# Centring the first block's tiles on VectorE before the turn, one mean from ScalarE, and a new order of the first loads, in an S5 + GEGLU layer

## The chip, the cores and the metric

The kernel runs on one core of one Trainium2 chip. Its engines are TensorE (PE; its weight loads are shown apart as PEld), VectorE (DVE), ScalarE (ACT), GpSimd (POOL) and SyncE (SP), which here only issues transfers. The metric is the device time of one execution in microseconds (us), the median of several runs.

## What is computed

One layer norm feeds two branches that are added to the input. `x` is 2048 x 512 in bf16. Cut to what matters:

```python
xn = (x - mean(x)) / sqrt(var(x) + eps)              # per row
dt = exp(log_dt); Lam_bar = exp(dt * Lam)            # 512 complex states
Bu = xn @ B_bar.T                                    # B_bar = ((Lam_bar - 1) / Lam) * B
h[t] = Lam_bar * h[t-1] + Bu[t]                      # scan over the 2048 rows
y = 2 * real(h @ C.T) + xn * Dskip
g = (gelu(xn @ w_gate) * (xn @ w_up)) @ w_down       # 512 -> 1376 -> 512
out = x + y + g
```

## The kernel before

The rows of x are cut into four blocks of 512 and each block into four tiles of 128 rows. Blocks 1 to 3 go one way: statistics and normalisation on VectorE, a transpose by DMA (`TR`), then matmuls with the transposed block: `GU` (gate and up), `BU` (into the states), the scan on VectorE (`CHAIN`) and `DN` (down projection and output).

Block 0 is handled apart so that TensorE has work early. Its gate and up products for the first 896 of the 1376 hidden columns (`GT_mm`, L693, matmuls at L703) use tiles that are only centred and turned on TensorE itself, not by DMA. The scale 1/std of a row is applied afterwards, as the factor `sc` of the gelu on ScalarE (L712) and of the product on VectorE (L715). The rest of block 0 uses the ordinary transposed block (`TR(0)`, L727, four DMA transposes issued on SP; then `GU(0)`, L828).

How tiles of block 0 were turned: for tiles 0 and 1 `raw_T` (L669) multiplies the uncentred tile by an identity, and `center` (L675) adds, in the same PSUM bank, a 512-column matmul of ones with a diagonal of negative means (`diag`, L928, on VectorE). Tiles 2 and 3 are centred on VectorE (`sub`, L932) and then turned by four PE transposes (`cent_T`, L686). In all cases ScalarE copies the turned tile out of PSUM to `XC` (L661). Ahead of this TensorE runs ten dummy matmuls of 512 columns (L918).

A tile's statistics are two VectorE instructions: L616 (bn_stats) and L617 (bn_aggr). `root` (L622 on VectorE, L623 and L624 on POOL) and `recip` (L628) make 1/std for two tiles at a time. `norms` (L635) writes the fully normalised tiles over the centred ones, and `TR(0)` waits for them.

The order on an engine comes from a scheduler inside the program: every operation is listed with a duration and its buffers, priorities are worked out backwards, and each engine's queue is fixed at build time. TensorE and SP keep the order of the listing. `ch` chains VectorE's first operations in a written order. A field `nb` forbids the scheduler to place an operation before a given time.

The first loads: SP issues the x tiles 0, 1 and 2, the first up chunk (columns 0 to 383), x tile 3, then the second and third gate and up chunks. ScalarE's queue issues the first gate chunk and three 1 KB parameter rows (L505). `load_par` (L519) on SP transposes the parameter rows after they have landed; its result feeds `params` (POOL's pow at L557 and the VectorE operations after it). Behind it on SP come the fourth gate and up chunk, `TR(0)`, x of block 1, the transposes of B, and so on. ScalarE also loads its table and runs a dummy gelu (L544) before its first copy.

Of the kernel before, what the change touches and what calls it, by code (L numbers as in the profile page):

```python
# [361 lines left out]
def d_pe(n_list):  # L362
    return sum(n / 2.4 + 2.5 for n in n_list)
# [3 lines left out]
def d_dve_ts4x(n): return 220.0 + 0.26 * n  # L367
D_TINY = 160.0
def d_act(n, ptr=0): return 190.0 + 0.833 * n + 90.0 * ptr
# [3 lines left out]
def build(nc, ins, out):  # L373
    with ExitStack() as es:
# [8 lines left out]
        def ring(parent, name, n):  # L383
            return [A.sub(parent, "%s%d" % (name, i), i) for i in range(n)]
# [74 lines left out]
        XCs = [[Buf("XC%d_%d" % (j, n), "xc", 2 * j + n, 2 * j + n + 1) for n in range(2)] for j in range(4)]  # L459
        ONE = A.alloc("ONE", [128], BF16, at=XC_all.hi)  # L460
        DG_all = A.alloc("DG", [2, 128], BF16, at=ONE.hi); DG = ring(DG_all, "DG", 2)
        H0_all = A.alloc("H0", [4, 896], BF16, at=SSb[2].lo); H0 = ring(H0_all, "H0_", 4)
# [15 lines left out]
        V(lambda e: e.memset(WRM.ap, 0.0), 150, [], [WRM], "wrm")  # L478
        half = V(lambda e: e.memset(HALF.ap, 0.5), D_TINY, [], [HALF], "half")  # L479
        V(lambda e: e.memset(PROW16.ap, 0.0), D_TINY, [], [PROW, *PROWq], "prow0")  # L480
        V(lambda e: e.memset(ONE.ap, 1.0), 250, [], [ONE], "one")

# [5 lines left out]
        def ld_w(W, Wc, src, ci, queue="sync", after=()):  # L488
            f0, f1 = FCH[ci]
            return S.dma(lambda e: e.dma_start(W.ap[:, :, f0:f1], src[:, f0:f1].rearrange("(k p) f -> p k f", p=128)),  # L490
                         512 * (f1 - f0) * 2, writes=[Wc[ci]], tag="ld_w", queue=queue, after=after)

        def ld_x0(j):
            S.dma(lambda e, j=j: e.dma_start(X[j].ap, x2[128 * j:128 * (j + 1), :]), 128 * 1024, writes=[X[j]], tag="ld_x0")
        ld_x0(0)
        ld_x0(1)
        ld_w(WG, WGc, ins["B_w_gate"], 0, "scalar", [half])
        ld_x0(2)
        ld_w(WU, WUc, ins["B_w_up"], 0)
        ld_x0(3)  # L500
        for ci in (1, 2):
            ld_w(WG, WGc, ins["B_w_gate"], ci)
            ld_w(WU, WUc, ins["B_w_up"], ci)
        for q, (nm, nb) in enumerate((("A_log_dt", 900.0), ("A_Lambda_re", 1300.0), ("A_Lambda_im", 1600.0))):
            S.dma(lambda e, q=q, nm=nm: e.dma_start(PROW.ap[4 * q:4 * q + 4, :], ins[nm].rearrange("(s p) -> s p", p=128)),  # L505
                  1024, writes=[PROWq[q]], tag="ld_" + nm, queue="scalar").nb = nb
        def late_loads():
# [5 lines left out]
        def load_T(bufs, nms):  # L513
            for b_, nm in zip(bufs, nms):
                S.dma(lambda e, b_=b_, nm=nm: e.dma_start_transpose(b_.ap, ins[nm]),
                      1.2 * 512 * 1024, writes=[b_], tag="tr_" + nm, issue=3000.0)

        def load_par():
            S.dma(lambda e: e.dma_start_transpose(PAR.ap.rearrange("p q t -> p (q t)").unsqueeze(1), PROW16.ap), 4096,  # L519
                  reads=PROWq, writes=[PAR], tag="tr_par", issue=900.0)  # L520

# [17 lines left out]
        POOL(lambda e: e.memset(HPI.ap, 0.5 * math.pi), 100, [], [HPI], "hpi")  # L539
        POOL(lambda e: e.iota(IOT.ap, [[1, 128]], base=0, channel_multiplier=-1), 300, [], [IOT], "iota")  # L540
        V(lambda e: e.tensor_scalar(IDN.ap, IOT.ap, 0.0, None, ALU.is_equal), d_dve_ts4x(128), [IOT], [IDN], "ident")
        POOL(lambda e: e.iota(IOTJ.ap, [[1, 512]], base=0, channel_multiplier=0), 600, [], [IOTJ], "iotj")
        SCR = A.alloc("SCR", [1], F32)
        ACT(lambda e: e.activation(SCR.ap, HALF.ap[:, 0:1], ACTF.Gelu_apprx_tanh), 200, [HALF], [SCR], "gelu0").nb = 1900.0  # L544
        POOL(lambda e: e.memset(HR.ap, 0.0), 300, [], HRp, "hr0")
        rstate = {"n": 0}
# [21 lines left out]
        W16p = [A.sub(A.alloc("W16v", [4, 4], F32, at=W16.lo), "W16_%d" % i, i) for i in range(4)]  # L568
        GATE = {"before_gelu": [], "nh": 0}
        sinT, sinP, cosT, cosP = (SC16.ap[:, 4 * i:4 * i + 4] for i in range(4))  # L570
# [82 lines left out]

        def xc_evac(j, bank, src, engs, after=()):
            for n, eng in enumerate(engs):
                per = KD // len(engs)
                dst = XC_all.ap[:, per * n:per * (n + 1), 128 * j:128 * (j + 1)]
                sr = src[:, 128 * per * n:128 * per * (n + 1)].rearrange("p (q t) -> p q t", q=per)
                w = [XCs[j][n]] if len(engs) == 2 else XCs[j]
                if eng == "A":  # L660
                    GATE["evTA"] = ACT(lambda e, sr=sr, dst=dst: e.activation(dst, sr, ACTF.Copy), d_act(128 * per), [BANK[bank]], w, "evT", after)  # L661
                else:
                    GATE["evT"] = V(lambda e, sr=sr, dst=dst: e.tensor_copy(dst, sr), 110 + 0.6 * 128 * per, [BANK[bank]], w, "evT", after)

        def raw_T(j, bank):
            def f(e):
                ins_ = None
                for k in range(KD):
                    ins_ = e.matmul(PS[bank][:, 128 * k:128 * (k + 1)], X[j].ap[:, 128 * k:128 * (k + 1)], IDN.ap,  # L669
                                    start=(k == 0), stop=False, skip_group_check=True)  # L670
                return ins_
            PE(f, 56.0 * KD, [X[j], IDN], [BANK[bank]], "T0")

        def center(j, bank, engs):
            PE(lambda e: e.matmul(PS[bank][:, :].rearrange("p (q t) -> p q t", q=KD), ONE.ap,  # L675
                                  DG[j].ap.unsqueeze(1).broadcast_to([128, KD, 128]), start=False, stop=True, skip_group_check=True),
               d_pe([512]), [ONE, DG[j], BANK[bank]], [BANK[bank]], "T0c")
            xc_evac(j, bank, PS[bank], engs)

        def cent_T(j, bank):  # L680
            pt = PS[bank].bitcast(BF16)

            def f(e):
                ins_ = None
                for k in range(KD):
                    ins_ = e.transpose(pt[:, 128 * k:128 * (k + 1)], XN[j].ap[:, 128 * k:128 * (k + 1)], IDN.ap)  # L686
                return ins_
            PE(f, 56.0 * KD, [XN[j], IDN], [BANK[bank]], "T0")
            xc_evac(j, bank, pt[:, 0:512], "A")

        FR = ((0, 192), (192, 384), (384, 640), (640, 896))

        def GT_mm(j, r, bank, us, ks=range(KD)):  # L693
            f0, f1 = FR[r]
            w = f1 - f0
            ci = max(0, r - 1)
            Wc = [(WGc, WUc)[u][ci] for u in us]
            dst = PS[bank][:, w * us[0]:w * (us[-1] + 1)].rearrange("p (w f) -> p w f", w=len(us))

            def f(e):  # L700
                ins_ = None
                for k in ks:
                    ins_ = e.matmul(dst, XCd(j, k), WGU[:, us[0]:us[-1] + 1, k, f0:f1], start=(k == 0), stop=(k == KD - 1))  # L703
                return ins_
            PE(f, d_pe([w * len(us)] * len(ks)), Wc + XCs[j][ks[0] // 2:ks[-1] // 2 + 1], [BANK[bank]], "GT")
# [204 lines left out]

        nwarm = 10
        wrm4 = WRM.ap.unsqueeze(1).broadcast_to([128, 4, 128])
        wb = next_bank()

        def fwarm(e, wb=wb):
# [3 lines left out]
            return ins_  # L919
        PE(fwarm, d_pe([512] * nwarm) * 1.6, [WRM], [BANK[wb]], "warm")  # L920
        tb = [next_bank(), next_bank()]
        tail_op = [None]

        def ch(*ops):
            for op in ops:
                tail_op[0] = S.order_behind(op, tail_op[0])
        def diag(j):
            return V(lambda e: e.tensor_scalar(DG[j].ap, IDN.ap, MVt[0][j].ap[:, 0:1], -1.0, ALU.mult, ALU.mult),  # L928
                     d_dve_ts4x(128), [IDN, MVt[0][j]], [DG[j]], "dg")

        def sub(j):
# [3 lines left out]
        load_W()  # L935
        for j in range(2):
            ch(*stats(0, j)); ch(diag(j))
        op, mn0, qb0, rq0 = root(0, 0, 2)
# [8 lines left out]

        raw_T(0, tb[0])
        center(0, tb[0], "AA")
        raw_T(1, tb[1])  # L950
        ub = {(j, r): next_bank() for j in range(2) for r in range(2)}
        for ks in ((0, 1), (2, 3)):
            for r in range(2):
                GT_mm(0, r, ub[0, r], [0], ks)
        center(1, tb[1], "A")
        def unit(j, r):
            bank = next_bank()
            GT_mm(j, r, bank, [0, 1])
            GT_evac(j, r, bank, rss[j])
        for j in range(2):  # L960
            if j:
                for r in range(2):
                    GT_mm(j, r, ub[j, r], [0])
                cent_T(2, tb[0])
            for r in range(2):
                GT_mm(j, r, ub[j, r], [1])
                GT_evac(j, r, ub[j, r], rss[j])
        unit(2, 0); unit(2, 1)
        unit(0, 2)
        cent_T(3, ub[0, 0])  # L970
        unit(1, 2)
# [97 lines left out]
```

## Time and profile before

| what | us |
|---|---|
| median of 7 runs | 179.28 |
| lowest and highest of them | 178.97, 179.51 |
| the profiled execution | 178.73 |
| its span, first to last instruction | 177.2 |
| TensorE busy in the span | 173.3 |
| VectorE busy | 159.0 |
| ScalarE busy | 88.8 |
| first GT matmul starts | 5.66 |
| first matmul of GU(0) starts | 18.88 |

Times inside the profile count from the start of the span. The chain of waits is followed back from the last instruction; each row names the engine, the line and how long the chain stayed there. A row of the timeline has the start, the time taken, engine and line, what is written and read, how many instructions are merged, and in brackets the idle time before it and what ended it. `ACTq` and `SPq` are the instruction queues that issue transfers; a transfer's landing comes later than its issue. The granted TensorE clock is 1.000 in the whole profile; matmuls at the very start are nevertheless seen twice as far apart as later ones of the same size.

### The profile page before, as it was taken

To read this page: it belongs to the slowest core of one execution; us is meant where nothing else is said; L and a number is where in the kernel's file an instruction comes from. 1 tells how busy PE (TensorE), PEld (TensorE's weight loads), DVE (VectorE), ACT (ScalarE), POOL (GpSimd) and SP (SyncE) were. 2 spreads that over 40 slices of the span, in tenths; PEclk is the share of its full clock that TensorE was granted. 3 is DMA by queue.
4 is the path that set the end of the run, shared out by engine and by line. 5 is a ranking of instruction groups with operands and counts; after the bars stand their busy time and mean duration, and the time that the engine had idled before them with its cause. 6 is when DMAs were issued, how large, how long until landed. Compare 5 with 4: busy or idle time off the path is not lost.

```text
span 177.2 us, 2501 instructions
## 1 busy us (share of the span) xinstructions
PE 173.3 (98%) x887; PEld 83.9 (47%) x887; DVE 159.0 (90%) x285; ACT 88.8 (50%) x167; POOL 10.1 (6%) x24
## 2 busy tenths in 40 slices
PE   7999999999999999999999999999999999999994
PEld 3754464444644444444644444444454444444453
DVE  4989999897999999779999999989999999999711
ACT  3475578998776898003676694000677770000000
POOL 3330240200000000300000000000000000000000
PEclk9999999999999999999999999999999999999999
DMA  5999986595999000011025000100001000000401
GB/s 156 334 298 108 251 232 125 96 153 110 147 252 304 0 4 2 0 52 67 4 41 107 0 2 0 33 30 30 30 0 30 4 0 0 0 0 30 139 31 43
DMA packets 33380, 14.36 MB, mean 81 GB/s; under 512 B 23672, under 2 KB 33368, under 8 KB 33368
## 3 DMA queue, kind: packets, MB, share of 16 engines
q1 hardware_dynamic: 32816, 13.81, 34.0%
q10 hardware_dynamic: 552, 0.40, 0.8%
q8 instruction: 7, 0.11, 0.3%
q14 instruction: 5, 0.04, 0.1%
HBM read 6.46 MB, written 2.10 MB: 48 GB/s over the span
## 4 chain that ended last, share of the span: by engine, by line
PE 98%; DVE 0%; ACT 0%; issue 0%
PE PS L868 37%; PE PS L828 32%; PE PS L739 16%; PE PS L703 7%; PE PS L802 3%; PE PS L918 2%; PE PS L686 0%; PE PS L675 0%; ACT arena L661 0%; DVE arena L886 0%; PE PS L669 0%; DVE arena L478 0%; DVE arena L479 0%
## 5 line engine op out<-in xcount | busy, mean ns | idle before, releaser
L868 PE MATMUL PS<-arena 128*128 128x512 bf16 (+3 forms) x323 | 66.2, 366 | 0.0
L828 PE MATMUL PS<-arena 128*128 128x512 bf16 x264 | 58.1, 379 | 0.0
L868 PEld LDWEIGHTS PS<-arena 128*128 128x128 bf16 (+1 forms) x323 | 30.8, 98 | 35.2
L828 PEld LDWEIGHTS PS<-arena 128*128 128x128 bf16 x264 | 25.8, 98 | 30.4
L772 DVE TENSOR_TENSOR_SCAN arena<-arena 128x512 bf16<-128x512 f32 x32 | 38.7, 1251 | 0.0
L843 ACT ACTIVATE arena<-PS 128x512 bf16<-128x512 f32 x33 | 19.8, 601 | 37.1 <-PE PS L828 32.6
L739 PE MATMUL PS<-arena 128*128 128x512 bf16 x128 | 28.1, 379 | 0.0
L846 ACT ACTIVATE arena<-PS 128x512 bf16<-128x512 f32 x33 | 19.8, 601 | 4.8 <-PE PS L828 4.7
L739 PEld LDWEIGHTS PS<-arena 128*128 128x128 bf16 x128 | 12.5, 98 | 14.9
L886 DVE TENSOR_TENSOR arena<-PS,arena 128x512 bf16<-128x512 f32 (+2 forms) x17 | 10.8, 652 | 8.9 <-PE PS L868 8.9
L860 ACT ACTIVATE PS<-arena 128x512 f32<-128x512 bf16 (+2 forms) x17 | 9.3, 581 | 17.4 <-DVE arena L886 16.7
L743 ACT ACTIVATE arena<-PS 128x512 bf16<-128x512 f32 x32 | 17.3, 595 | 1.3 <-PE PS L739 1.3
L848 DVE TENSOR_TENSOR arena<-arena 128x512 bf16<-128x512 bf16 x33 | 13.1, 411 | 1.7 <-ACT arena L846 1.7
L703 PE MATMUL PS<-arena 128*128 128x192 bf16 (+2 forms) x80 | 13.1, 315 | 0.4 <-ACT arena L661 0.3
L616 DVE BATCH_NORM_STATS2 arena<-arena 128x6 f32<-128x512 bf16 x16 | 10.2, 680 | 1.7 <-DMA arena<-in_A_x_dram 1.7
L759 DVE TENSOR_TENSOR arena<-arena 128x4096 bf16<-128x4096 bf16 (+1 forms) x5 | 9.2, 1858 | 0.7 <-ACT arena L611 0.7
L703 PEld LDWEIGHTS PS<-arena 128*128 128x128 bf16 x80 | 7.0, 98 | 5.6 <-ACT arena L661 0.7
L761 DVE TENSOR_TENSOR arena<-arena 128x4096 bf16<-128x4096 bf16 (+1 forms) x5 | 9.2, 1857 | 0.0
L785 DVE TENSOR_TENSOR arena<-arena 128x4096 bf16<-128x4096 bf16 x4 | 9.1, 2281 | 0.0
L784 DVE TENSOR_TENSOR arena<-arena 128x4096 bf16<-128x4096 bf16 x4 | 9.1, 2280 | 0.0
L712 ACT ACTIVATE arena<-PS,arena 128x192 bf16<-128x192 f32 (+1 forms) x16 | 6.8, 447 | 3.5 <-PE PS L703 1.8
L715 DVE SCALAR_TENSOR_TENSOR arena<-PS,arena 128x192 bf16<-128x192 f32 (+1 forms) x16 | 6.7, 443 | 0.7 <-ACT arena L712 0.7
(85 smaller groups left out, 109.0 us busy)
## 6 DMA issues: line engine op xcount, KB each, us to landing
out_dram<-arena SPq DMA_DIRECT2D x15, 128.0 KB, 1.7
arena<-in_A_x_dram SPq DMA_DIRECT2D x3, 512.0 KB, 4.7
arena<-in_B_w_down_dram SPq DMA_DIRECT2D x1, 1280.0 KB, 7.0
arena<-in_A_x_dram SPq DMA_DIRECT2D x4, 128.0 KB, 3.6
arena<-in_B_w_gate_dram SPq DMA_DIRECT2D x2, 256.0 KB, 4.9
arena<-in_B_w_up_dram SPq DMA_DIRECT2D x2, 256.0 KB, 5.3
arena<-in_B_w_gate_dram SPq DMA_DIRECT2D x1, 480.0 KB, 4.0
arena<-in_B_w_up_dram SPq DMA_DIRECT2D x1, 480.0 KB, 4.7
```

The source lines that it names most:

```text
L616: return (V(lambda e: e.bn_stats(ST[tt].ap, X[tt].ap), d_dve_1x(512), [X[tt]], [ST[tt]], "bnst"), V(lambda e: e.bn_aggr(MVt[b][j].ap, ST[t ...
L703: ins_ = e.matmul(dst, XCd(j, k), WGU[:, us[0]:us[-1] + 1, k, f0:f1], start=(k == 0), stop=(k == KD - 1))
L739: ins_ = e.matmul(PS[bank][:, :], BBT[c][dk].ap[:, 128 * s:128 * (s + 1)], XNT[b].ap[:, dk, :], start=(dk == 0), stop=(dk == KD - 1))
L743: ACT(lambda e, bank=bank, k3=k3, s=s, c=c: e.activation(SSc[k3][s][c].ap, PS[bank][:, :], ACTF.Copy), d_act(512), [BANK[bank]], [SSc[k3][ ...
L772: V(lambda e, g=g, rb=rb, init=init: e.tensor_tensor_scan(g.ap, rb, g.ap, init, ALU.mult, ALU.add), d_dve_scan(512), [g, PA[RRr]] + ([CARc ...
L828: ins_ = e.matmul(PS[bank][0:m, c0:c1], W.ap[:, dk, 128 * ft:128 * ft + m], XNT[b].ap[:, dk, c0:c1], start=(dk == 0), stop=(dk == KD - 1))
L843: GATE["last_gelu"] = ACT(lambda e, bg=bg, kk=kk, m=m: e.activation(GG[kk].ap[0:m, :], PS[bg][0:m, :], ACTF.Gelu_apprx_tanh), d_act(512), ...
L846: ACT(lambda e, bu=bu, kk=kk, m=m: e.activation(UPB[kk].ap[0:m, :], PS[bu][0:m, :], ACTF.Copy), d_act(512), [BANK[bu]], [UPB[kk]], "evU")
L848: V(lambda e, kk=kk, m=m, ft=ft, k2=k2: e.tensor_tensor(HTt[k2][ft].ap[0:m, :], GG[kk].ap[0:m, :], UPB[kk].ap[0:m, :], ALU.mult), d_dve_tt ...
L860: ACT(lambda e: e.activation(PS[bank][:, c0:c1], X[tt].ap[:, c0:c1], ACTF.Copy), d_act(c1 - c0), [X[tt]], [BANK[bank]], "seed")
L868: ins_ = e.matmul(PS[bank][:, c0:c1], l_[:, 128 * j:128 * (j + 1)], r_[:, c0:c1], start=False, stop=last and n == len(ops) - 1, skip_group ...
L886: V(lambda e: e.tensor_tensor(OUTB[ko].ap[:, c0:c1], PS[bank][:, c0:c1], XD[tt].ap[:, c0:c1], ALU.add), d_dve_1x(c1 - c0), [BANK[bank], XD ...
```

## The change

- `raw_T`, `center`, `diag` and their buffers go. Tiles 0 and 1 are now centred on VectorE and turned by `cent_T`, as tiles 2 and 3 were. Tile 0 is turned into two PSUM banks, two 128-column transposes each, with one ScalarE copy for each bank. Tile 2 still has one copy, tiles 1 and 3 too.
- The mean of tile 1 comes from ScalarE: an activation over the tile with scale -1/512 whose sum goes to `NM1`. VectorE adds `NM1` to the tile without waiting for the tile's statistics, and these follow after it. The activation's other output goes to a buffer that is overwritten later.
- On TensorE both tiles are turned before the first GT matmul, and the gate matmuls of tile 1 come before the up matmuls of tile 0.
- Seven dummies instead of ten, and two small fillers of 128 columns after them.
- The first gate chunk is loaded in two halves (input rows 0 to 255 and 256 to 511). ScalarE's queue issues the first, after the identity is made; SP issues the second, behind x tile 1. A GT matmul group on two of the four row groups waits only for its half.
- The three parameter rows move from ScalarE's queue to SP, behind the third up chunk; their transpose moves behind the fourth gate and up chunk.
- The identity is made earlier, the clearing of `PROW` moves from VectorE to POOL, and the dummy gelu may be placed earlier (its `nb` goes from 1900 to 900).

The built order shows, beside this, that VectorE's table and coefficient operations take other places between 10 and 30 us; the order of TensorE after the first block's GT matmuls and the order on SP after `TR(0)` stay as they were.

The core of the diff:

```diff
-        for q, (nm, nb) in enumerate((("A_log_dt", 900.0), ("A_Lambda_re", 1300.0), ("A_Lambda_im", 1600.0))):
-            S.dma(lambda e, q=q, nm=nm: e.dma_start(PROW.ap[4 * q:4 * q + 4, :], ins[nm].rearrange("(s p) -> s p", p=128)),
-                  1024, writes=[PROWq[q]], tag="ld_" + nm, queue="scalar").nb = nb
+        def load_par():
+            for q, nm in enumerate(("A_log_dt", "A_Lambda_re", "A_Lambda_im")):
+                S.dma(lambda e, q=q, nm=nm: e.dma_start(PROW.ap[4 * q:4 * q + 4, :], ins[nm].rearrange("(s p) -> s p", p=128)),
+                      1024, writes=[PROWq[q]], tag="ld_" + nm)
...
         ld_x0(0)
         ld_x0(1)
-        ld_w(WG, WGc, ins["B_w_gate"], 0, "scalar", [half])
+        ld_wg0(0, "scalar", [GATE["ident"]])
+        ld_wg0(1, "sync")
         ld_x0(2)
...
-        nwarm = 10
+        nwarm = 7
...
         load_par()
         load_W()
-        for j in range(2):
-            ch(*stats(0, j)); ch(diag(j))
+        tr_par()
+        ACT(lambda e: e.activation(H0[3].ap[:, 0:D], X[1].ap, ACTF.Copy, scale=-1.0 / D, accum_out=NM1.ap), d_act(512) + 90,
+            [X[1]], [H0[3], NM1], "mean1")
+        ch(*stats(0, 0)); ch(sub(0))
+        ch(V(lambda e: e.tensor_scalar(XN[1].ap, X[1].ap, NM1.ap, None, ALU.add), d_dve_ts4x(512), [X[1], NM1], [XN[1]], "sub"))
+        ch(*stats(0, 1))
...
-        raw_T(0, tb[0])
-        center(0, tb[0], "AA")
-        raw_T(1, tb[1])
+        fill(2)
+        cent_T(0, tb, "AA")
+        cent_T(1, [wb])
         ub = {(j, r): next_bank() for j in range(2) for r in range(2)}
         for ks in ((0, 1), (2, 3)):
             for r in range(2):
                 GT_mm(0, r, ub[0, r], [0], ks)
-        center(1, tb[1], "A")
...
+        for r in range(2):
+            GT_mm(1, r, ub[1, r], [0])
         for j in range(2):
-            if j:
-                for r in range(2):
-                    GT_mm(j, r, ub[j, r], [0])
-                cent_T(2, tb[0])
             for r in range(2):
                 GT_mm(j, r, ub[j, r], [1])
                 GT_evac(j, r, ub[j, r], rss[j])
+                if j == 0 and r == 0:
+                    cent_T(2, tb)
         unit(2, 0); unit(2, 1)
+        cent_T(3, [ub[0, 0]])
         unit(0, 2)
-        cent_T(3, ub[0, 0])
```

## The prediction

> **What bounds the kernel now.** I read the engine totals first, then the chain that ended last, then the opening stretch instruction by instruction. The totals and the chain's summary, from the page:
>
> ```profile
> PE 173.3 (98%) x887; PEld 83.9 (47%) x887; DVE 159.0 (90%) x285; ACT 88.8 (50%) x167; POOL 10.1 (6%) x24
> ...
> PE 98%; DVE 0%; ACT 0%; issue 0%
> ```
>
> TensorE is the chain. Whatever starts its stream of real matmuls earlier is worth that much at the end, as long as nothing behind it becomes late. The chain of waits over the first 20 us (start, length, what):
>
> ```profile
> 0.99 3.67 PE PS L918 x10
> 4.66 0.22 PE PS L669 x4
> 4.88 0.23 PE PS L675
> 5.11 0.02 issue
> 5.14 0.39 ACT arena L661
> 5.53 0.14 issue
> 5.66 0.82 PE PS L703 x8
> 6.48 0.22 PE PS L675
> 6.70 1.52 PE PS L703 x16
> ...
> 11.70 7.34 PE PS L703 x36
> ```
>
> The ten dummies (L918) end at 4.5, turning (L669) and centring (L675) of tile 0 follow, ScalarE copies it out (L661), and the first gate matmul starts at 5.66. From there to the first matmul of GU(0), which starts at 18.88, the chain never leaves TensorE for long. The timeline of VectorE and ScalarE in the same stretch (start, length):
>
> ```profile
> 2.87 0.69 DVE L616 BATCH_NORM_STATS2 arena<-arena 128x6 f32<-128x512 bf16 x1 [1.17 <-DMA arena<-in_A_x_dram]
> 3.04 1.28 ACT L544 ACT_TABLE_LOAD   x1 [3.04 <-issue]
> 3.60 0.18 DVE L617 BATCH_NORM_AGGREGATE arena<-arena 128x2 bf16<-128x6 f32 x1
> 4.62 0.69 DVE L616 BATCH_NORM_STATS2 arena<-arena 128x6 f32<-128x512 bf16 x1 [0.56 <-DMA arena<-in_A_x_dram]
> 6.75 0.35 DVE L932 TENSOR_SCALAR arena<-arena 128x512 bf16<-128x512 bf16 x1
> ```
>
> Tile 0 lands at 2.84, tile 1 only at 4.60: its transfer shared the engines with the 384 KB gate chunk. Last, the SP queue, which issues nearly all transfers in order:
>
> ```profile
> 4.73 0.97 SPq L490 DMA_DIRECT2D arena<-in_B_w_up_dram  x1
> 6.80 1.18 SPq L519 DMA_TRANSPOSE arena<-arena  x1
> 8.03 0.57 SPq L490 DMA_DIRECT2D arena<-in_B_w_gate_dram  x1
> 8.64 0.50 SPq L490 DMA_DIRECT2D arena<-in_B_w_up_dram  x1
> 9.19 6.47 SPq L727 DMA_TRANSPOSE arena<-arena  x4
> ```
>
> The four L727 transposes are TR(0); the last is issued at 13.54 and lands at 17.20. GU(0) needs all four at 18.88, so they have 1.7 us to spare. After that the tightest wait of TensorE is 1.2 us (L802 at 44.37, on ScalarE's copies) and 1.4 us (L739 at 32.28, on the last transpose of TR(1), landed at 30.87). A lead below 1.2 us can pass through to the end.
>
> **The change, part by part.**
>
> *Dummies, ten to seven.* They start 0.43 us apart up to 3.52 and 0.22 us apart from 3.85, the clock having risen after 2.86 us of work. Seven last at most 7 x 0.427 = 2.99 us, to 3.98, and the two 128-column fillers to about 4.2. They then end no later than tile 0 is centred, so they are off the path. The trace covers the rise: 2.99 us of dummies against 2.86 us, a margin of 0.13 us. The Trainium skill's "TensorE: Matmul & The Clock Gate", Part 1, wants some 3.4 us of sustained work in a free-running window, and its Part 4 says that transposes do not count as busy. By that page the seven are too few and the sum would be that of the clock rival below; by the row they suffice and cost nothing. I take the row.
>
> *Tile 0.* Statistics at 2.87 and 3.60, then sub(0) in place of the diagonal at 3.81. Its row is 0.35 us (L932), so it is done at 4.16. The transposes start at 4.21 and cost 4 x 0.055 as the L686 rows do; the first pair is out at 4.21 + 0.11 + 0.17 = 4.49.
>
> *Mean of tile 1 on ScalarE.* The first gate half is issued behind ident, which ends near 1.7: 1.77 to 2.24. The three parameter loads leave ScalarE's queue, so the table load moves from 3.04 to 2.27 and, with the 0.20 us dummy, is done at 3.77. The Trainium skill's "ScalarE: Activation LUTs", What ACT_TABLE_LOAD costs, adds a drain of some 1.4 us to a table switch; here the next instruction began 0.01 us after the load. By the page the lead found below would turn into a loss of 0.6 us, by the row the drain is not there. The mean needs tile 1. Its 128 KB now go before both gate halves on the same queue; tile 0's row is 2.1 us from issue to landing, so 1.19 + 2.1 = 3.3, and at worst the old 4.60. No row has an activation with a sum. Nearest: 0.60 us (L661, 512 columns) with nothing added, 0.91 us with the 0.71 us of L593 and a further 0.20 us 128x1 activation. I take 0.70, near L593's: 3.79 to 4.49. Queued behind the mean on ScalarE are tile 0's copies, behind sub(1) on VectorE all later statistics, so a late mean delays both.
>
> *Order of the front.* sub(1) at 4.52 to 4.87; its four transposes 4.92 to 5.14. They stand ahead of every gate matmul, so TensorE waits here. ScalarE copies tile 0's halves from 4.51 and 4.79 (0.38 us each, rows 5.14 and 5.42), done at 4.89 and 5.17. The gate halves hold 192 KB each; at the 370 GB/s of 3.25 to 4.5 they need 1.04 us from about 2.9, and with 0.4 us from last byte to semaphore they land near 4.4 (before: 4.96). So the first gate matmul starts at 5.14, against 5.66.
>
> *From there.* 8 at 0.0825: 5.80. The tile 1 gate matmuls need its copy: 5.33 + 0.60 = 5.93, start 5.98, a wait of 0.18, end 6.64. Four up matmuls: 6.97 (the up chunk landed at 6.58 before and has no more bytes ahead of it). The transposes of tile 2 need sub(2). VectorE has sub(1) and no diagonals: bn(1) at 4.79, bn(2) at 5.81 (before: 5.82), sub(2) done at 7.10. So TensorE waits 0.17 and goes on at 7.14: T 0.22, 12 up matmuls 0.99, eight 384s 1.31, T 0.22, four 512s 0.86 and the last 36 in 7.35 give 18.09. Lead: 18.88 - 18.09 = 0.79 us; with the mean at 0.60 or 0.91 us, 0.89 or 0.58. Cross-check: the earlier start 0.52, one centring matmul 0.22 (the other lay before 5.66) and the old waits before 6.63, 7.39 and 9.13 (0.36) are saved, 0.35 of new waits given back: 0.75.
>
> *Parameter loads to SP.* This is what I weigh most. They stood on ScalarE's queue at 1.77 to 3.0 and landed by 6.70. Now they are behind the last of the four 256 KB chunks (wu2, issued at 4.73, landed at 10.30). A transfer queued right behind it, the parameter transpose, landed 0.18 us later (6.80 + 3.7 = 10.48). So the parameters land at about 10.3 (10.0 to 10.55), and the parameter transpose, which waits for them, goes at 10.4 instead of 6.80. Queued behind it on SP: TR(0), x of block 1, both B transposes, TR(1). It blocks until 11.6; TR(0) follows at 1.31 us each, the last issued at 15.55. Landing takes 2.5 us from issue in the median row of L727, 3.66 us in the fourth one of before, which met a stall of the transfers (62 and 7 GB/s at 14 to 16 us). By the median: 18.05; by the other: 19.2. The stall should be over by 15.55, so I take 18.2. TensorE is ready at 18.09: GU(0) starts at about 18.25, **0.63 us earlier**. Cover gone: the 1.7 us are used up.
>
> Further on SP, x of block 1 moves from 15.71 to about 17, landing at 20.9; VectorE asked for it at 20.85. The B transposes, landed at 22.57 and 24.24, come about 1.3 later; BU(0) needs the first at 24.7 and the second 3.4 us after that. TR(1) waited for VectorE until 24.50 with SP idle since 23.2, so it absorbs this. The parameter transpose's data now queue behind the last gate and up chunks (landed at 13.35 before), so POOL's pow waits until about 13.2, not 10.5; behind it on POOL is nothing needed before 22, and VectorE reaches its first use after 13.5. No cost. Half loads, memsets and ident on POOL/VectorE: hidden by the 1.2 us in which VectorE waited for tile 0.
>
> **Sum.** The profiled execution took 178.73 us, of which 177.2 is span; minus 0.63 gives 178.1. It lies 0.55 below the median of the runs, 179.28, so the median should become 179.28 - 0.65 = 178.63.
>
> **The rivals.**
> - *TR(0) late, slower.* Parameters at 10.55 and the fourth transpose at 3.66 us: GU(0) starts at 15.8 + 3.66 + 0.06 = 19.5, 0.6 late: 179.9. It decides from a landing after 18.88 on; below it only eats gain. For it: every step of it is in SP's order. Against: the stall ended at 16.
> - *TR(0) halfway, or tile 1 not earlier.* Landing at 18.6 to 19.2, or tile 1 still at 4.60: then the mean ends at 5.32, sub(2) at 7.9, and the same sum gives 18.92. Either way about 179.2. Against the second: the gate chunk no longer comes first.
> - *Clock.* If the seven dummies fall short, the first gate matmuls run at half speed until 2.9 us of them are done: 1.45 lost, 0.8 net: 180.1. The margin is 0.13 us.
> - *Front faster and TR(0) on time*: lead up to 1.0, 178.3.
>
> **How the numbers follow.** Forecast with the fast end 0.67; halfway or tile 1 late 0.18; TR(0) late 0.09; clock 0.06. A measurement of this kernel tells about 0.2%, 0.36 us, from no change. Faster 0.67, within 0.18, slower 0.15. The range goes from 178.2 (lead 1.0 and a little) to 179.7, which leaves out most of the slow cases and little at the low end.
>
> **What would show it.** Right: first gate matmul at 5.0 to 5.3; table load at 2.3; tile 1 landed by 3.8; the parameter transpose issued near 10.4; GU(0) at 18.1 to 18.4 and no TensorE wait after it. Wrong: the parameter transpose much earlier (gain limited by the front alone) or later than 11; GU(0) waiting for a transfer beyond 18.9; dummies or first gate matmuls at double spacing after 4.2.

## The result and the profile after

The changed kernel is slower: median 180.61 us (179.66 to 183.1 over 12 runs) against 179.33 us (178.75 to 179.97 over 31 runs) for the kernel before on the same chip. The ratio is 1.0069 [1.0055, 1.0084]. The forecast was 178.63. The run of 183.1 us had a granted clock of 0.991, and the ratio leaves it out. The profiled execution took 180.85 us, its span 179.0.

The page of the changed kernel, engine totals and the chain's summary:

```profile
PE 173.0 (97%) x884; PEld 84.2 (47%) x884; DVE 160.7 (90%) x283; ACT 89.4 (50%) x169; POOL 10.3 (6%) x25
...
PE 92%; DVE 2%; DMA 2%; ACT 1%; issue 0%; ACTq 0%; POOL 0%; DVEq 0%; POOLq 0%
```

TensorE is as busy as before (173.0 us against 173.3), but the chain now leaves it: 92% instead of 98%. So the time is waiting, not work. The waits of TensorE in the first 40 us (line, released by; total, times, longest):

```profile
PE PS L823 <- DMA arena<-arena: 2.2, 1, 2.2
...
PE PS L673 <- DVE arena L939: 0.6, 1, 0.6
```

L823 is the first matmul of GU(0), and what it waits for is a DMA transpose. The chain over the same stretch (start, length, what) says where the two waits stand:

```profile
1.10 1.21 DVE arena L480
...
2.78 1.28 ACT L554
...
4.28 0.62 ACT arena L936 x2
...
5.41 0.61 PE PS L673 x4
6.02 1.85 PE PS L698 x20
...
16.92 0.48 DVE arena L710
17.40 3.46 DMA arena<-arena
20.86 0.14 issue
21.00 5.12 PE PS L823 x23
```

The front of the chain is the identity on VectorE (L480), ScalarE's table load (L554), the mean (L936) and the turning of tile 1 (L673). The chain counts a step from the end of the one before it; by the trace's own rows the first gate matmul starts at 5.81, against 5.66 before and 5.14 in the forecast. TensorE is ready for GU(0) at 18.65, only 0.23 us ahead of the old 18.88. But the fourth transpose of TR(0), issued at 17.40, lands at 20.86, and GU(0) starts at 21.00: 2.12 us later than before. The chain puts VectorE (L710) ahead of that issue; but the last tile of block 0 was normalised by 12.72, and SP's issue before it ended at 17.36, so the fourth transpose waited for SP itself. Every later TensorE block in the chain is late by the same 2.12 us (the last long one starts at 143.88, before at 141.76), and the span is 1.8 longer.

SP's queue in the changed kernel (start and length of the issue):

```profile
5.25 0.92 SPq L491 DMA_DIRECT2D arena<-in_B_w_up_dram  x1
6.21 0.94 SPq L515 DMA_DIRECT2D arena<-in_A_log_dt_dram  x1
...
11.07 1.18 SPq L519 DMA_TRANSPOSE arena<-arena  x1
12.30 6.37 SPq L722 DMA_TRANSPOSE arena<-arena  x4
18.71 0.58 SPq L485 DMA_DIRECT2D arena<-in_A_x_dram  x1
...
26.31 5.29 SPq L722 DMA_TRANSPOSE arena<-arena  x4
```

SP's wait ahead of the parameter transpose (the third parameter row; total, times, longest):

```profile
SPq L340 <- DMA arena<-in_A_Lambda_im_dram: 2.2, 1, 2.2
```

The third up chunk (issued at 5.25) landed at 10.96 and the parameter rows behind it by 10.98. The parameter transpose (L519) was issued at 11.07, before at 6.80. Everything behind it on SP up to TR(1) is issued 1.8 to 3.9 us later: TR(0) starts at 12.30 instead of 9.19, x of block 1 goes at 18.71 instead of 15.71, TR(1) at 26.31 instead of 24.50.

**Theory A**: the new place of the parameter rows makes the parameter transpose late, and SP's order hands that to TR(0) and TR(1); the loss is TensorE waiting for the one or the other. **Theory B**: the front alone is to blame (late clock, late identity, ScalarE's mean, fewer dummies), and TR(0) is late only by chance.

### The profile page after: what moved, and what is told of

The parts are those of the page before. It is cut to its first block, busy times and chain, and to the rows that moved or that the text cites. A ratio compares the mean times of both kernels' runs of the same rounds, so it can differ in the third digit from the quotient of the medians.

```text
span 179.0 us, 2505 instructions
## 1 busy us (share of the span) xinstructions
PE 173.0 (97%) x884; PEld 84.2 (47%) x884; DVE 160.7 (90%) x283; ACT 89.4 (50%) x169; POOL 10.3 (6%) x25
## 4 chain that ended last, share of the span: by engine, by line
PE 92%; DVE 2%; DMA 2%; ACT 1%; issue 0%; ACTq 0%; POOL 0%; DVEq 0%; POOLq 0%
PE PS L863 37%; PE PS L823 32%; PE PS L734 15%; PE PS L698 4%; PE PS L797 3%; DMA arena<-arena 2%; DVE arena L710 1%; ACT L554 1%; DVE arena L480 1%; PE PS L673 1%; ACT arena L936 0%; ACT arena L707 0%; ACTq L499 0%; DVE arena L939 0%; DVE arena L612 0%
## 5 line engine op out<-in xcount | busy, mean ns | idle before, releaser
L863 PE MATMUL PS<-arena 128*128 128x512 bf16 (+3 forms) x323 | 66.2, 366 | 0.0
L823 PE MATMUL PS<-arena 128*128 128x512 bf16 x264 | 58.1, 379 | 2.2 <-DMA arena<-arena 2.2
L863 PEld LDWEIGHTS PS<-arena 128*128 128x128 bf16 (+1 forms) x323 | 30.8, 98 | 35.2
L823 PEld LDWEIGHTS PS<-arena 128*128 128x128 bf16 x264 | 25.7, 98 | 32.8 <-issue 2.6
L710 DVE SCALAR_TENSOR_TENSOR arena<-PS,arena 128x192 bf16<-128x192 f32 (+1 forms) x16 | 6.9, 449 | 0.9 <-ACT arena L707 0.4
```

The lines of the kernel that those rows point to most:

```text
L823: ins_ = e.matmul(PS[bank][0:m, c0:c1], W.ap[:, dk, 128 * ft:128 * ft + m], XNT[b].ap[:, dk, c0:c1], start=(dk == 0), stop=(dk == KD - 1))
L863: ins_ = e.matmul(PS[bank][:, c0:c1], l_[:, 128 * j:128 * (j + 1)], r_[:, c0:c1], start=False, stop=last and n == len(ops) - 1, skip_group ...
```

## The experiments

Edits are against the changed kernel unless it is said otherwise; "before" in a ratio is the kernel before on the same chip.

**The rows early on SP** (e1): the three loads go ahead of the second gate chunk.

```diff
         ld_x0(3)
+        load_par()
         for ci in (1, 2):
...
-        load_par()
         load_W()
```

> The changed kernel with one thing moved: the three parameter rows are issued on SP before the second gate chunk, not behind the third up chunk. Theory A (the rows wait in the transfer queue behind the weight chunks, so their transpose holds SP until 11.1 us and TR(0) lands at 20.9, after TensorE is ready at 18.6): the rows land by about 8, the parameter transpose goes right behind the fourth chunks near 9, TR(0) lands by 18, TensorE waits less than 0.2 us at GU(0), and the time falls by 1.3 to 1.9 us against the changed kernel, to 179.0 to 179.3. Rival B (the stall of the transfers between 14.5 and 17 us delays TR(0) whatever stands before it): TR(0) still lands at 19.5 or later, 180.0 or more. Rival C (the front itself is slower, by the late clock and the late identity): no more than 0.3 us gained.

Measured: 178.52 us, ratio 0.9967 [0.9937, 0.9997]. The median is 2.1 us below the changed kernel's, more than expected. The ratio counts all runs, two of which took 180.40 and 180.98; the medians alone give 0.994. SP's queue in this run:

```profile
3.67 0.37 SPq L511 DMA_DIRECT2D arena<-in_A_log_dt_dram  x1
...
8.72 1.27 SPq L520 DMA_TRANSPOSE arena<-arena  x1
10.04 5.18 SPq L723 DMA_TRANSPOSE arena<-arena  x4
15.26 0.58 SPq L485 DMA_DIRECT2D arena<-in_A_x_dram  x1
```

The rows landed by 7.58, TR(0) by 16.44, and TensorE waits neither at GU(0), which starts at 18.60, nor at BU(1). The front is as in the changed kernel: first gate matmul at 5.80, dummies seven, mean on ScalarE. Theory A holds: the loss goes when the three 1 KB loads go ahead, with the front unchanged.

**Only the rows late** (e2): the kernel before, with the rows on SP behind the third up chunk and their transpose behind the fourth chunks.

```diff
-                  1024, writes=[PROWq[q]], tag="ld_" + nm, queue="scalar").nb = nb
+                  1024, writes=[PROWq[q]], tag="ld_" + nm)
...
-        load_par()
         load_W()
+        load_par()
```

> The kernel before with only the parameter rows moved to SP behind the third up chunk and their transpose behind the fourth chunks, as the change has it; turning, dummies, mean and gate chunk stay. Theory A: the parameter transpose is issued at 10.4 to 11, TR(0) lands at 19.5 to 20.9, GU(0) waits 0.7 to 2.1 us, time 180.0 to 181.2. Rival C (the front is at fault): 179.1 to 179.5, as before.

Measured: 180.06 us, ratio 1.0032 [1.0017, 1.0047]: slower, at the lower edge of what was expected, and at another place. The parameter transpose was issued at 10.74, TR(0) landed at 18.36, and GU(0) was not late. The wait of TensorE stood at BU(1):

```profile
PE PS L739 <- DMA arena<-arena: 1.3, 1, 1.3
```

The chain of this run shows what leads there:

```profile
17.19 4.14 DMA arena<-in_A_x_dram
...
21.35 1.28 DVE arena L616 x2
...
30.15 3.51 DMA arena<-arena
...
33.90 2.10 PE PS L739 x9
```

x of block 1 is issued at 17.19 instead of 15.71 and lands at 21.33 instead of 19.85. VectorE had asked for it at 20.85, so the spare was 1.0 us, and its statistics start 0.5 late. The rest comes in two steps: x of block 2, 512 KB, is issued at 25.71 instead of 22.77, since the issue of the second B transpose took 3.92 us instead of 2.40 and held SP until 25.05, and the first transpose of TR(1) right behind it lands at 31.76, 0.7 after that x; and the last transpose, issued at 30.15 instead of 28.36, takes 3.5 us to land instead of 2.5. The chain goes through VectorE, but there the first tile for TR(1) was normalised by 24.98, and SP came to it only at 26.19 and issued the four without a gap.

**The turn behind TR(0)** (e3): the rows stay late, but their transpose is listed after TR(0).

```diff
         load_W()
-        tr_par()
...
         TR(0)
+        tr_par()
```

> The changed kernel with the parameter transpose listed behind TR(0) on SP; the rows stay where the change put them. Theory A: SP no longer waits for the rows ahead of TR(0), TR(0) is issued from 9.9 on as the normalised tiles come and lands by 17, GU(0) starts at 18.6 without a wait, 179.0 to 179.3, if the parameters, then there at 17 to 18 instead of 14, are still early enough for the tables of the scan; if not, a wait shows at BU(1), DN(0) or the scan and the time stays above 179.6. Rival B: TR(0) lands after 19 all the same.

Measured: 180.21 us, ratio 1.0048 [1.0024, 1.0071]. TR(0) was issued from 9.27 and GU(0) started at 18.59 without a wait, so this edit removes the wait by the same mechanism. It gives the time back later: TensorE waits once, at 110.19 (L863, the down projection), 1.1 us for VectorE. The chain ahead of it is VectorE without a gap, the scan and what follows it. That VectorE gets its tables later here, and is late for that reason, is argued from the chain and was not tried by itself.

**The identity alone** (e4): POOL's 512-wide iota and memset are put behind the identity.

```diff
-        POOL(lambda e: e.iota(IOTJ.ap, ...), 600, [], [IOTJ], "iotj")
-        POOL(lambda e: e.memset(HR.ap, 0.0), 300, [], HRp, "hr0")
+        S.order_behind(POOL(lambda e: e.iota(IOTJ.ap, ...), 600, [], [IOTJ], "iotj"), GATE["ident"])
+        S.order_behind(POOL(lambda e: e.memset(HR.ap, 0.0), 300, [], HRp, "hr0"), GATE["ident"])
```

> The changed kernel with POOL's 512-column iota and the clearing of HR ordered behind the identity, so that POOL does nothing large beside it. The identity took 1.20 us in the changed kernel and 0.60 before. If POOL's work beside it is what lengthens it: 0.3 to 0.4 us, ScalarE's first gate half at 1.5, the mean of tile 1 done near 4.2 instead of 4.9, the first gate matmul at 5.0 to 5.3 instead of 5.8. By theory A the time hardly moves (180.4 to 180.8), since TR(0) and not the front ends the wait at GU(0); by rival C it falls by 0.5 or more.

Measured: 180.63 us, ratio 1.0055 [1.0033, 1.0077]: nothing gained. The identity's instruction, in the changed kernel and then in this one (start, length):

```profile
1.10 1.20 DVE L480 TENSOR_SCALAR arena<-arena 128x128 bf16<-128x128 int32 x1 [0.16 <-POOL arena L479]
```

```profile
1.10 0.23 DVE L480 TENSOR_SCALAR arena<-arena 128x128 bf16<-128x128 int32 x1 [0.16 <-POOL arena L479]
```

The front does get better: the mean ends at 4.09 instead of 4.90 and the first gate matmul starts at 5.21. A wait of 0.7 us for the up chunk (landed at 7.44) takes part of that, GU(0) starts at 18.81, and then TensorE waits 0.2 us for the first B transpose and 1.4 us at BU(1):

```profile
PE PS L734 <- DMA arena<-arena: 1.4, 1, 1.4
...
PE PS L698 <- DMA arena<-in_B_w_up_dram: 0.7, 1, 0.7
```

A better front is worth nothing while SP is late. Theory B falls with this run and e1: the changed kernel, e2 and e4 have three different fronts and end at 180.61, 180.06 and 180.63 us, and e1 has the changed kernel's front and ends at 178.52.

**Both** (e5): the edits of e1 and e4 together.

> The changed kernel with both single edits: the parameter rows before the second gate chunk, and POOL's large operations behind the identity. With the rows early no wait follows the front, so what the front gains should now reach the end. Theory A with the late identity as the second cost: first gate matmul at 5.2 instead of 5.8, but the first up chunk landed at 7.4 in the run with the identity first (6.8 in the changed kernel) and held TensorE for 0.7 us; so GU(0) at 18.5 to 18.8 and 178.3 to 178.7. If the front is worth what the prediction said (0.8 us of lead): 178.0 or less.

Measured: 178.36 us, ratio 0.9938 [0.9916, 0.996], the first version clearly below the kernel before. First gate matmul at 5.17, no TensorE wait after the front. GU(0) starts at 18.73, no earlier than in e1 (18.60): in this profile the clock rose only at 6.75.

**The halves undone** (e10): e5 with the first gate chunk as one transfer on ScalarE's queue.

```diff
-        ld_wg0(0, "scalar", [GATE["ident"]])
-        ld_wg0(1, "sync")
+        ld_w(WG, WGc, ins["B_w_gate"], 0, "scalar", [GATE["ident"]])
...
-            if ci == 0 and us == [0] and len(ks) == 2:
-                Wc = [WG0h[ks[0] // 2]]
```

> The kernel with the rows early and the identity first, with the first gate chunk in one transfer on ScalarE's queue behind the identity instead of two halves. The chunk then lands whole, near 5.0 to 5.4, instead of 4.5 and 5.0 for the halves. If the halves matter: the first gate matmul moves from 5.17 to 5.4 or later and 0.2 us or more are lost. If the up chunk bounds: within 0.2 us of 178.36.

Measured: 178.24 us, ratio 0.9943 [0.9924, 0.9961]: as fast as e5. The first gate matmul of its profile starts at 5.58 instead of 5.17, and the time does not follow. Cutting the chunk brings nothing that shows.

**The mean on VectorE** (e7: e1 without ScalarE's mean; e9: e5 without it). Tile 1 is centred with VectorE's own statistics.

```diff
-        ACT(lambda e: e.activation(H0[3].ap[:, 0:D], X[1].ap, ACTF.Copy, scale=-1.0 / D, accum_out=NM1.ap), d_act(512) + 90,
-            [X[1]], [H0[3], NM1], "mean1")
...
-        ch(V(lambda e: e.tensor_scalar(XN[1].ap, X[1].ap, NM1.ap, None, ALU.add), d_dve_ts4x(512), [X[1], NM1], [XN[1]], "sub"))
-        ch(*stats(0, 1))
+        ch(*stats(0, 1)); ch(sub(1))
```

> The early-rows kernel with tile 1 centred by VectorE's own statistics (stats, then the subtraction), without ScalarE's mean. Tile 1 lands at 3.4; statistics at 4.1 to 5.0, the subtraction at 5.0 to 5.4: the same time as with ScalarE's mean, which ended at 4.90 in the changed kernel. So the first gate matmul stays within 0.1 us and the time within 0.2 us: ScalarE's mean brings nothing as it stands. If it does bring what the prediction assigned to it, 0.3 us or more slower.

Measured for e7: 178.67 us, ratio 0.9972 [0.9945, 0.9998], against 0.9967 for e1. The centring starts at 5.04 instead of 5.00. With the identity late, ScalarE's mean brings nothing.

> The kernel with the rows early and the identity first, with tile 1 centred by VectorE's own statistics, without ScalarE's mean. There ScalarE's mean was done at 4.12 and the subtraction began at 4.25; VectorE's own statistics let it begin near 5.04. If that matters: first gate matmul at 5.8 instead of 5.17, 0.2 to 0.6 us slower than 178.36. If the landing of the first up chunk (7.0 to 7.4) bounds the front anyway: within 0.2 us of 178.36.

Measured for e9: 178.47 us, ratio 0.9978 [0.9947, 1.001], which does not tell it from before. Its twelve runs fall into two groups: eight at 178.33 to 178.62, four at 180.03 to 180.43. The profiled one (180.19) is of the second group, and its chain shows where this one lost its time:

```profile
5.51 0.61 PE PS L674 x4
6.12 3.20 PE PS L699 x20
9.32 0.43 PE PS L674 x4
```

The same twenty gate matmuls take 1.85 us in the changed kernel's chain. Here they run at half speed until 9.61.

**Dummies** (e6: e1 with ten; e8: the kernel before with seven).

```diff
-        nwarm = 7
+        nwarm = 10
```

> The early-rows kernel with ten dummies instead of seven. In the four profiles with seven the TensorE clock rose at 5.3 to 6.2 us, in the two with ten at 3.7. If the number of dummies decides: the rise is at 3.7, the dummies end near 4.5, the first gate matmul is at 5.65 as tile 1 allows, and the time falls by 0.2 to 0.4. If the rise comes at a phase that no kernel sets: it may fall anywhere from 3.7 to 6.2, and the time stays within 0.2 us of 178.5, or rises by up to 0.4 where ten cold dummies last to 5.3.

> The kernel before with seven dummies instead of ten and nothing else. If the dummies hold the turning of tile 0 (it began at 4.50, straight behind them, with tile 0 there since 2.84 and its mean at 4.08): the turning starts at 3.9 to 4.0 and the first gate matmul, bound by the gate chunk's landing at 4.96, at 5.1 to 5.4, and 0.2 to 0.5 us are gained. If the clock's rise hangs on the dummies, it comes after 5 us, the turning and first gate matmuls run at half speed and the gain is gone: 179.3 or more.

Measured: e6 178.93 us, ratio 0.9971 [0.9955, 0.9988]; e8 178.87 us, ratio 0.9971 [0.9955, 0.9986]. Fewer dummies alone give the kernel before about 0.5 us. In e6 all ten dummies ran 0.427 us apart, so ten did not bring the clock up earlier; its first gate matmul starts at 6.43.

**A second profile of each of the two kernels** (e11: before; e12: after).

> The kernel before, unchanged: one more profile. In the profile that the prediction was made from, the clock rose at 3.74 and the time was 178.73, 0.6 below the median. In the eight profiles of changed kernels taken since, ten dummies or seven, it rose at 5.3 to 6.8 in all but one. If the rise comes at a phase that no kernel sets, this profile may show it late; then ten dummies last to 5.2, the first gate matmul starts near 6.5 and the time is near 179.4 to 179.9.

Measured for e11: 179.93 us. Its chain's start:

```profile
0.99 4.45 PE PS L918 x10
...
12.90 7.34 PE PS L703 x36
```

The same ten dummies took 3.67 us in the profile that the forecast was made from, and the last 36 gate and up matmuls started there at 11.70. One rise of the clock, 1.2 us: the first profile was a favourable one, and nearly all runs of the kernel before lie between the two (178.7 to 180.0).

> The changed kernel, unchanged: one more profile. Theory A: the parameter transpose is again issued at 10.9 to 11.3 and all SP work up to TR(1) is 1.5 us or more late; whether the wait stands at GU(0) (if transfers stall between 14.5 and 17 us) or at BU(1) (if not) may differ, the sum is 1.3 to 2.2 us.

Measured for e12: 180.64 us. The parameter transpose was issued at 11.30 and TR(1) from 26.64. TensorE waited 0.4 us for the up chunk, 0.9 us at GU(0) and 0.7 us at BU(1). The two late waits are 1.6 us in all, as expected, against 2.2 us at GU(0) alone in the first profile. TR(0) had landed by 19.79 and TR(1) by 33.92, 0.35 and 0.25 us before these matmuls start; the view of waits names VectorE and ScalarE as the last to end them, so that the transposes alone held them is not shown here.

## Why the prediction was wrong, step by step

- **"Parameter loads to SP" is the step that failed**, twice. First its size at TR(0). The rows were put at 10.0 to 10.55; they landed at 10.98, since the third up chunk itself came at 10.96, not 10.30. The step said "The stall should be over by 15.55, so I take 18.2". The fourth transpose landed at 20.86 and 19.79 in the two profiles. In both the issue of one of the transposes ahead of it grew, to 2.45 and 2.10 us instead of 1.27, so the fourth was issued at 17.40 and 17.28, not at 15.55. The 2.66 us between 18.2 and 20.86 are three terms: TR(0) began at 12.30 instead of 11.6 (0.70), the fourth issue came 5.10 us behind the first instead of 3.95 (1.15), and it took 3.46 us to land instead of 2.65 (0.81). The trace of before had the second term: its fourth issue took 2.12 us (13.54 to 15.66), and the forecast counted only its late landing. The stall of the transfers did not stay at its old time: it lay at about 15.5 to 17 in the changed kernel.
- **"TR(1) waited for VectorE until 24.50 with SP idle since 23.2, so it absorbs this ... No cost"** is the larger error of reasoning. e2 and e4 show it alone: with GU(0) on time, the wait appears at BU(1), 1.3 and 1.4 us. SP's 1.3 us of idle time was real, but it was that of one profile. In e2 SP is 1.48 us late at x of block 1 and, behind the longer issue of the second B transpose, 2.94 us late at x of block 2; the idle time takes up 1.25 us of that, and TR(1) starts 1.69 us late. In the changed kernel's first profile it is VectorE that holds TR(1): it waits for x of block 1, which SP issues 3.00 us later, begins its statistics at 22.81 instead of 20.85, and TR(1) goes out at 26.31, 1.81 us late, right behind the first normalised tile (26.28). So part of the delay comes back through VectorE, out of the same queue. The forecast had even read the spare (TR(1) at 30.87 against 32.28, 1.4 us) and not compared it with its own 1.3 us shift plus what follows.
- **The rival "TR(0) late, slower"** named the mechanism, with 0.09 and 179.9; it was too cheap by 0.7 us, since it had no longer issue in it, and too unlikely, since it needed only one of two landings to be late. Two of the forecast's own signs of being wrong came: the parameter transpose after 11 (11.07), and GU(0) waiting for a transfer beyond 18.9.
- **The lead at GU(0)** was put at 0.79 us; 0.23 was measured against the same 18.88. Tile 1 landed at 3.38 (3.3 forecast), the mean took 0.71 us (0.70), and the gelu began 0.01 us after the table load, so the drain that the Trainium skill's "ScalarE: Activation LUTs", What ACT_TABLE_LOAD costs, describes does not show here either. What missed is what the mean waits for: the identity took 1.20 us, not the 0.59 of the trace of before, so the first gate half was issued at 2.33 and the table load at 2.78, not 2.27. (The last line of the forecast's sum takes off 0.65 where its own result was 0.63.)
- **The clock.** Seven dummies were said to suffice by 0.13 us. The clock rose at 6.17 in the changed kernel. But the rise is not set by the number of dummies (e6, e11), and the runs before probably hold late rises too, as e11 does. So against the median the front is worth more than against the one profile: the median of e1 lies 1.0 us below the 179.56 of before on the same chip. The Trainium skill's "TensorE: Matmul & The Clock Gate", Part 1, speaks of a free-running window of some 3.4 us. The rises of all profiles but e9's lie from about 3.7 to 6.8 us, within one such window, and agree with it; e9's 9.61 lies beyond. The forecast was wrong to set it aside for one row.
- **Right**: dummies off the path, tile 0's centring, the two added centrings on VectorE, the order on SP.

Of the change's parts, the order of the front, fewer dummies and the rows off ScalarE's queue are together worth about 1 us once the rows are issued early (e1, e5, e10); fewer dummies alone gave 0.5 (e8), the rest was not split. ScalarE's mean and the halves bring nothing that these runs can tell, beside the second group of e9's times. The best version is e10, 178.24 us, with e5 level.

Open: what stalls the transfers at 14 to 17 us and lengthens an issue. A single 16 KB packet that the profile lists as an instruction packet takes 1.35 to 1.48 us of it in the traces of before and after. The fourteen profiles tell more. Of their 56 TR(0) issues 52 take 1.19 to 1.32 us and four take 2.10 to 2.45 us, one each in before, after, e10 and e12. In each of these four a 16 KB packet begins while the issue runs. It does so in one other, in e7, 0.35 us before the issue's end; there the next issue, x of block 1, takes 1.11 us instead of 0.58. In the rest this packet begins later, up to 23.20 us, and in the kernel before alone at 13.74 and at 19.85. So the two go together and their place changes from run to run; that the packet is the cause was not tried. The loss is therefore known by place and by origin, and its exact split between the shift and the stall is not.

## What to carry to other kernels

A small load moved behind large ones on the same queue landed with the last of them (10.98 and 10.96 us), and the issue that waited for it held the whole queue: follow every later entry of that queue to its reader, and compare each shift with that reader's spare. An idle stretch of one profile absorbs a delay only as far as it is still there in the next, and less where what ends it comes out of the same queue. Where the first microseconds depend on a clock that rises at another time in each run, look at two profiles before taking a start time from one.

## What the runs showed that was not expected

- **The clock's rise wanders**: 3.74 and about 6.4 us in two profiles of the kernel before; 6.17 and 4.42 in two of the changed one; 5.78, 5.25, 5.41, 6.75, 6.50, 9.61 and 4.03 in its variants with seven dummies (e1, e3, e4, e5, e7, e9, e10). Where the record of the clock has no rise, the spacing of the matmuls shows it: about 3.7 in e2 and 6.1 in e6, with ten dummies, and 6.3 in e8, with seven. The granted clock of 1.000 given ahead does not show this. The records show full clock in stretches of 170.67 or 174.08 us, 3.41 apart. In e9, where TensorE is idle for 0.6 us ahead of tile 1's turn, four runs of twelve are some 1.8 us longer. e1 and e7 have the same idle time and two such runs each; e5 has none of either, and neither has e6, with ten dummies, but e10 has 0.5 us of idle time and no such run. Only e9's profile shows a late rise in such a run.
- **One VectorE instruction, three lengths**: the 128x128 conversion of the identity takes 0.23 us without, and 0.59 or 1.20 us beside, POOL's iota and memset of 512 columns. In the changed kernel it ends at 2.30, just after POOL's memset (2.21).
- **An activation with a sum is two instructions**: 0.61 us for 512 columns and 0.19 us to read the accumulator, 0.71 us in all.
